# The statistics pass of the gate/up loop, moved from in front of a unit's evacuation to behind it

## The chip, the cores and the metric

The kernel runs on one core of one Trainium2 chip. The metric is the device time of one execution in microseconds (us), smaller is better. Executions of one kernel spread over 4.6 us here (the fastest of the kernel before took 765.78 us, the slowest 770.36 us), so differences of 0.2% need several rounds.

## The reference

Only the second half matters here: a gated feed-forward block whose two wide matrix products, gate and up, form the loop that the change edits. Shapes: 2048 tokens, D = 1024, F = 3584, all bf16.

```python
def _B_ref(x, w_gate, w_up, w_down):
    g = _silu(x @ w_gate)
    u = x @ w_up
    return (g * u) @ w_down

xn = _layernorm(A_x)
s = _A_ref(xn, A_wqkv, A_wo)            # linear attention block
g = _silu(_B_ref(xn, B_w_gate, B_w_up, B_w_down))
return A_x + s * g
```

## The kernel before

The feed-forward products use a Strassen-like scheme with seven products in place of eight. It needs differences of weight blocks in fp16, and these are scaled by a power of two so that they fit. The scale comes from a *statistics pass* over the raw weight tile: ScalarE squares it and sums per partition (`emit_st0`), TensorE adds over the partitions with a matrix of ones (`emit_st1`), VectorE makes the scale and applies it (`emit_st2`), GpSimd forms the four differences and writes the prepared tile to HBM for the second pass over the tokens (`emit_T`).

```python
def emit_st0(key, t):                                   # ScalarE
    asum = stp.tile([P, 1], BF16, name="asum", tag="asum")
    ...                                                 # cut: junk is a free part of the tile
    nc.scalar.activation(out=junk, in_=raw_view(key, t), func=ACT.Square, accum_out=asum[:])

def emit_a(key):                                        # first four products of a unit, then s1..s3
    ...
    nc.scalar.activation(out=s1[:], in_=x_[:], func=ACT.Copy, scale=rc)      # "the s1 copy", L752
    ...

def emit_evac(key, h, tail=None):                       # evacuation of a unit
    p, kind, fg = key
    ...
    if kind == "g":
        ...
        nc.scalar.activation(out=sg[:, 3, :], in_=s3[:], func=ACT.Silu)            # L799
        nc.scalar.activation(out=sg[:, 0, :], in_=x_[:], func=ACT.Silu, scale=rc)  # L800
        nc.scalar.activation(out=sg[:, 1:3, :], in_=cf[:], func=ACT.Silu)          # L801
    else:
        ...                                             # VectorE only
```

Units alternate: even i is a gate unit (`"g"`), odd i an up unit (`"u"`), 28 units of about 6.07 us. The loop of the first pass, cut to the order of issue:

```python
keys = [(p, kd, fg) for fg in range(NFG) for kd in ("g", "u")]
n = len(keys)                                           # 28

def raw(j):
    return 0 <= j < n and keys[j] in raw_keys           # not prepared in an earlier stage

def pipe(j):                                            # the statistics pass
    if raw(j):
        emit_st0(keys[j], w_tiles[keys[j]])
...
for i in range(n):
    load_w_to(...)                                      # cut
    if i + 1 < n:
        emit_a(keys[i + 1])
        emit_c22(keys[i + 1])
    for j in (range(5) if i == 0 else (i + 4,) if i != n - 6 else ()):
        pipe(j)
    if first:
        wd_pipe(i)          # down weights: a Square (i % 3 == 1) or a Copy that scales (i % 3 == 0)
        ...
    mb = emit_b(keys[i])                                # last three products of the unit
    if first and i in range(6, 11):
        io_load(mb)                                     # small loads of x and s for much later
    pipe1(i + (4 if i == n - 5 else 3), i)              # ones-matmul of the pass of a unit ago
    ...
    emit_evac(keys[i], h, tail if i == n - 1 else None)
    pipe2(i + (4 if i == n - 5 else 3))                 # scale and differences
    ...
```

All gate weights and up group 0 are prepared in an earlier stage of the kernel (`NPREP = 13` and the two first keys), so the raw keys are the 13 up keys 3, 5, ..., 27.

Of the kernel before, what the change touches and what calls it, by code (L numbers as in the profile page):

```python
# [21 lines left out]
def kernel(  # L22
# [179 lines left out]
    def raw_view(key, t):  # L202
        return wd_q(t)[:, 0:4:3, :] if key[1] == "w" else t[:, 0].rearrange("p a b -> p (a b)")
# [30 lines left out]
    def kcol(key):  # L234
        return 2 * NFG + key[2] if key[1] == "w" else 2 * key[2] + (1 if key[1] == "u" else 0)
# [7 lines left out]
    def emit_st0(key, t):  # L243
        asum = stp.tile([P, 1], BF16, name="asum", tag="asum")
        with nc.allow_low_precision("a bound that only sets a power of two"):
            junk = wd_q(t)[:, 1:3, :] if key[1] == "w" else t[:, 1].rearrange("p a b -> p (a b)")
            nc.scalar.activation(out=junk, in_=raw_view(key, t), func=ACT.Square, accum_out=asum[:])  # L247
        st_tiles[key] = asum

    def emit_st1(key, ps):  # L250
        nc.tensor.matmul(ps, lhsT=ones[:], rhs=st_tiles.pop(key)[:], start=True, stop=True, skip_group_check=True)
        st_tiles[key] = ps
# [459 lines left out]
    with ExitStack() as p3:  # L712
# [19 lines left out]
        def rc_of(key):  # L732
            if key[1] == "u" and key[0] != passes[0]:
                return rcl[:, key[2]:key[2] + 1]
            return rc_all[:, kcol(key):kcol(key) + 1]
# [45 lines left out]
        def emit_evac(key, h, tail=None):  # L781
            p, kind, fg = key
            x_, zw, s2, s3, _, *c = grp.pop(key)
            rc = rc_of(key)
            if kind == "g":
                cf = m4.tile([P, 2, TB], FP32, name="cg", tag="m4")
                d12 = cf[:]
            else:
                c = c[0]
                d12 = c[:, 0:2, :]  # L790
                sg = sg_tiles.pop((p, fg))
                nc.vector.scalar_tensor_tensor(out=h[:, 2 * fg, 0:TB], in0=x_[:], scalar=rc, in1=sg[:, 0, :],
                                               op0=ALU.mult, op1=ALU.mult)
            nc.vector.scalar_tensor_tensor(out=d12, in0=zw[:], scalar=rc,  # L794
                                           in1=s2[:, None, :].to_broadcast([P, 2, TB]), op0=ALU.mult, op1=ALU.add)
            if kind == "g":
                sg = m4.tile([P, 4, TB], BF16, name="sg", tag="m4")
                sg_tiles[(p, fg)] = sg
# [4 lines that stand above are left out]
                if tail is not None:  # L803
                    tail()
                hv = h[:, 2 * fg:2 * fg + 2, :].rearrange("p a b -> p (a b)")
                nc.vector.tensor_tensor(out=hv[:, TB:4 * TB], in0=c[:].rearrange("p a b -> p (a b)"),
                                        in1=sg[:, 1:4, :].rearrange("p a b -> p (a b)"), op=ALU.mult)
# [259 lines left out]
        for pi, p in enumerate(passes):  # L1067
            h = hp.tile([P, FC, TB2], BF16, name="hT", tag="hT")
            keys = [(p, kd, fg) for fg in range(NFG) for kd in ("g", "u")]
            n = len(keys)  # L1070
            first = pi == 0
            last_pass = pi == NPASS - 1

            if first:
                first_gate[0] = marks[("S", NB - 1, 0)]

            def raw(j):
                return 0 <= j < n and keys[j] in raw_keys

            def pipe(j):  # L1080
                if raw(j):
                    emit_st0(keys[j], w_tiles[keys[j]])

            def pipe1(k, i):
                if raw(k):
                    emit_st1(keys[k], grp[keys[i + 1]][4][:, 0:1])

            def pipe2(j):
                if raw(j):
                    t = w_tiles[keys[j]]  # L1090
                    emit_st2(keys[j], t, later=j == n - 1)
                    emit_lk(keys[j][2])
                    if j < n - 1:
                        emit_T(keys[j], t)
                    raw_keys.discard(keys[j])

            wd_live = {}

            def wd_pipe(i):
                if (i - 3) % 3 == 0 and i // 3 - 1 in wd_live:  # L1100
                    key, t = wd_live[i // 3 - 1]
                    w = raw_view(key, t)
                    nc.scalar.activation(out=w, in_=w, func=ACT.Copy, scale=cs_all[:, kcol(key):kcol(key) + 1])
                if (i - 1) % 3 == 0 and (i - 1) // 3 in wd_live:
                    emit_st0(*wd_live[(i - 1) // 3])

            def wd_pipe1(i):
                if (i - 2) % 3 == 0 and (i - 2) // 3 in wd_live:
                    emit_st1(wd_live[(i - 2) // 3][0], grp[keys[i + 1]][4][:, 1:2])

            def wd_pipe2(i):
                m, r = divmod(i + 1, 3)
                if r == 1 and m - 1 in wd_live:
                    emit_T(*wd_live[m - 1])
                elif r == 0:
                    if m - 1 in wd_live:
                        emit_st2(*wd_live[m - 1], later=True)
                    if NWE + m < NFG:
                        t = w_slot()
                        load_wd(t, NWE + m)  # L1120
                        wd_live[m] = ((p, "w", NWE + m), t)

            def more_S(m):
                if first:
                    scale_h(h, 2 * m, nc.scalar)
                    scale_h(h, 2 * m + 1, nc.vector)
                emit_hs(h, 0, m, nc.vector)

            def next_S(m):
                emit_hs(h, 1, m, nc.vector)  # L1130

            def tail():
                emit_hs(h, 0, 2, nc.vector)
                if first:
                    scale_h(h, 7, nc.scalar)
                emit_hs(h, 0, 3, nc.vector)

            na0 = 6 if first else 8
            load_w_to(base + na0)
            if first:  # L1140
                wd_pipe2(-1)
            emit_a(keys[0])
            emit_c22(keys[0])
            first_gate[0] = None
            for i in range(n):
                load_w_to(base + i + (na0 if i < n - 7 else 8 if i > n - 6 or not first else 7))
                if i + 1 < n:
                    emit_a(keys[i + 1])
                    emit_c22(keys[i + 1])
                for j in (range(5) if i == 0 else (i + 4,) if i != n - 6 else ()):  # L1150
                    pipe(j)
                if first:
                    wd_pipe(i)
                    for k in {n - 4: (0,), n - 3: (2, 4), n - 2: (5, 6)}.get(i, ()):
                        scale_h(h, k, nc.scalar)
                mb = emit_b(keys[i])
                if first and i in range(6, 11):
                    io_load(mb)
                pipe1(i + (4 if i == n - 5 else 3), i)
                if first:  # L1160
                    wd_pipe1(i)
                if i == n - 2:
                    emit_hs(h, 0, 0, nc.gpsimd)
                if i == n - 1:
                    emit_hs(h, 0, 1, nc.vector)
                emit_evac(keys[i], h, tail if i == n - 1 else None)
                pipe2(i + (4 if i == n - 5 else 3))
                if first:
                    wd_pipe2(i)
                    if i == 5:  # L1170
                        emit_lk(0)
                    if i == n - 5:
                        emit_lam()
                    elif i == n - 4:
                        emit_sc(keys[-1], w_tiles[keys[-1]])
                        emit_T(keys[-1], w_tiles[keys[-1]])
                        scale_h(h, 1, nc.vector)
                    elif i == n - 3:
                        scale_h(h, 3, nc.vector)
                if deferred:  # L1180
                    deferred.pop(0)()
            base += n
            emit_down(p, h, base, last_pass, more_S, next_S)
            base += 2 * NWA
# [32 lines left out]
```

## Time and profile before

| | before |
|---|---|
| median of the first 3 runs | 767.11 us (766.46 to 768.77) |
| span of the profiled execution | 767.3 us |
| TensorE (PE) busy | 754.1 us, 98% |
| ScalarE (ACT) busy | 345.8 us, 45% |
| PE gaps in the first gate/up loop | 1.15 us, one gap |

What to look for are the gaps of the busiest engine, and what ends them. From the page of the kernel before, part 1 (busy us of each engine) and part 4 (the chain that ended last):

```profile
PE 754.1 (98%) x3717; PEld 349.6 (46%) x3717; DVE 551.5 (72%) x1076; ACT 345.8 (45%) x473; POOL 287.4 (37%) x413
...
PE 92%; DVE 4%; ACT 1%; DMA 1%; issue 1%; SPq 0%; ACTq 0%; DVEq 0%
```

PE sets the time. The windows view of the kernel before, three stretches of the loop (length, then busy us and instructions of PE, PEld, DVE, ACT and POOL, then granted clock, DMA share, GB/s):

```profile
300.00:320.00 20.00, 20.00 (x96) 9.06 (x94) 17.21 (x28) 14.19 (x16) 17.62 (x18) 1.00 0.82 286
320.00:340.00 20.00, 18.85 (x90) 8.46 (x89) 15.11 (x28) 10.69 (x15) 10.47 (x12) 1.00 1.02 376
340.00:360.00 20.00, 20.00 (x97) 9.06 (x96) 16.45 (x27) 14.40 (x17) 18.20 (x19) 1.00 0.69 240
```

PE is full but for 1.15 us between 320 and 340 us, where the DMA engines are busiest of the three (share 1.02, against 0.82 and 0.69). The only wait of PE there, from the waits view of the kernel before (waiter, what it waited for, us in total, times, longest):

```profile
PE xb L725 <- ACT sg L800: 1.1, 1, 1.1
```

Two pieces of the ScalarE timeline of the kernel before (start, us, engine, line, operation; in brackets the idle time before it and what ended it). L247 is the statistics pass, L1103 the scaling Copy of down weights, L752 the s1 copy, L799 to L801 the Silus:

```profile
275.71 0.67 ACT L752 ACTIVATE s<-xb,rc_all 128x512 f32<-128x512 f32 x1
276.28 1.90 ACT L247 ACTIVATE w_sb<-w_sb 128x2048 bf16<-128x2048 bf16 x1
278.08 0.19 ACT L247 ACTIVATION_READ_ACCUMULATOR w_sb<-w_sb 128x1 bf16 x1
278.17 1.99 ACT L1103 ACTIVATE w_sb<-w_sb,cs_all 128x2048 bf16<-128x2048 bf16 x1
281.31 0.69 ACT L752 ACTIVATE s<-xb,rc_all 128x512 f32<-128x512 f32 x1 [1.15 <-PE xb L725]
...
324.23 0.67 ACT L752 ACTIVATE s<-xb,rc_all 128x512 f32<-128x512 f32 x1
330.63 1.91 ACT L247 ACTIVATE w_sb<-w_sb 128x2048 bf16<-128x2048 bf16 x1 [5.72 <-DMA w_sb<-in_B_w_up_dram]
332.44 0.19 ACT L247 ACTIVATION_READ_ACCUMULATOR w_sb<-w_sb 128x1 bf16 x1
332.54 0.67 ACT L752 ACTIVATE s<-xb,rc_all 128x512 f32<-128x512 f32 x1
333.11 1.99 ACT L1103 ACTIVATE w_sb<-w_sb,cs_all 128x2048 bf16<-128x2048 bf16 x1
335.00 0.62 ACT L799 ACTIVATE sg<-s 128x512 bf16<-128x512 f32 x1
335.52 0.67 ACT L800 ACTIVATE sg<-xb,rc_all 128x512 bf16<-128x512 f32 x1
```

The first piece is up unit 3: the pass, the Copy, then 1.15 us of idle until PE has the next operand. No Silu follows before that, because an up unit has none. The second piece is up unit 11: ScalarE stands in front of the pass for 5.72 us until the weights of key 15 have landed. The s1 copy behind it is late, and so is the Silu of L800, which frees a PSUM buffer that PE waits for. ScalarE ran nothing that stood behind the pass in those 5.72 us: the s1 copy came right after the pass, at 332.54 us, 8.31 us after the last one, where it is 5.60 us in the first piece.

### The profile page before, as it was taken

The numbers are of one execution on the slowest core, as the hardware profiler recorded it, in microseconds if no ns is written. First come the engines' busy times: TensorE is split into PE (matmuls) and PEld (weight loads), VectorE is DVE, ScalarE is ACT, GpSimd is POOL, SyncE is SP. The second block draws the span as 40 slices with busy tenths as digits, with TensorE's granted clock in tenths as the row PEclk, the third lists the DMA queues.
The fourth block names the chain that finished last, engine by engine and source line by source line (L and its number), as shares of the span: only waits on it lengthen the run. The fifth ranks groups of instructions, "written<-read, shape, count | busy, mean of one in ns | idle before, by whom it ended". The sixth has DMA issues, their size and how long they took to land.

```text
span 767.3 us, 10482 instructions
## 1 busy us (share of the span) xinstructions
PE 754.1 (98%) x3717; PEld 349.6 (46%) x3717; DVE 551.5 (72%) x1076; ACT 345.8 (45%) x473; POOL 287.4 (37%) x413
## 2 busy tenths in 40 slices
PE   7999999999999999999999999999999999999996
PEld 3544444444444444444444444444444444444443
DVE  6788557997666588878889885358676776787335
ACT  3545667788853566566447411132323223201111
POOL 0477499959685255858656000110000000200000
PEclk9999999999999999999999999999999999999999
DMA  9945868769889769898888227399654444530923
GB/s 308 352 95 114 229 221 274 248 222 259 237 304 262 256 228 312 283 333 298 308 309 290 89 81 262 113 356 334 229 185 167 165 169 175 187 114 23 296 73 117
DMA packets 105396, 170.29 MB, mean 222 GB/s; under 512 B 34688, under 2 KB 82176, under 8 KB 94720
## 3 DMA queue, kind: packets, MB, share of 16 engines
q1 hardware_dynamic: 94960, 121.00, 50.3%
q0 software_dynamic: 7936, 44.31, 15.0%
q10 hardware_dynamic: 2448, 4.33, 1.6%
q8 instruction: 29, 0.48, 0.3%
q14 instruction: 23, 0.19, 0.1%
HBM read 111.67 MB, written 50.59 MB: 211 GB/s over the span
## 4 chain that ended last, share of the span: by engine, by line
PE 92%; DVE 4%; ACT 1%; DMA 1%; issue 1%; SPq 0%; ACTq 0%; DVEq 0%
PE zw L725 25%; PE kv_ps L486 14%; PE dzw L910 13%; PE xb L725 12%; PE s_ps L659 7%; PE yb L725 6%; PE dx L910 6%; PE q_ps L170 4%; PE dy L910 3%; PE kvz L508 1%; DMA xp<-in_A_x_dram 1%; DVE o_blk L640 1%; PE nd_ps L632 1%; DVE pqT L141 1%; DVE pqT L153 0%
## 5 line engine op out<-in xcount | busy, mean ns | idle before, releaser
L725 PEld LDWEIGHTS <-w_sb 128*128 128x128 f16 (+1 forms) x1568 | 152.2, 98 | 184.3 <-issue 1.7
L725 PE MATMUL xb<-xnT,w_sb 128*128 128x512 bf16 x448 | 115.0, 379 | 1.1 <-ACT sg L800 1.1
L486 PE MATMUL kv_ps<-wkv_sb,xnT 128*128 128x512 bf16 x512 | 115.5, 383 | 0.4 <-DVE xnT L473 0.2
L725 PE MATMUL zw<-xnT,w_sb 128*128 128x512 bf16 x448 | 105.8, 379 | 0.0
L725 PE MATMUL zw<-S,w_sb 128*128 128x512 f16 x448 | 105.8, 379 | 0.0
L280 POOL TENSOR_TENSOR w_sb<-w_sb 128x512 f16<-128x512 bf16 x42 | 48.9, 1165 | 96.7 <-DVE w_sb L268 36.3
L247 ACT ACTIVATE w_sb<-w_sb 128x2048 bf16<-128x2048 bf16 x42 | 79.9, 1902 | 9.1 <-DMA w_sb<-in_B_w_up_dram 7.1
L910 PE MATMUL dx<-w_sb,hT 128*128 128x512 bf16 x224 | 82.8, 379 | 0.0
L486 PEld LDWEIGHTS <-xnT 128*128 128x128 bf16 x512 | 49.0, 98 | 57.2 <-issue 2.4
L910 PEld LDWEIGHTS <-hT 128*128 128x128 bf16 (+1 forms) x448 | 43.8, 98 | 52.9
L910 PE MATMUL dzw<-w_sb,hT 128*128 128x512 f16 (+1 forms) x224 | 64.4, 379 | 0.0
L170 PE MATMUL q_ps<-xnT,wq_sb 128*128 128x512 bf16 x256 | 58.2, 379 | 0.0
L753 DVE SCALAR_TENSOR_TENSOR s<-yb,rc_all,s 128x512 f32<-128x512 f32 x42 | 31.5, 749 | 37.0 <-ACT s L752 37.0
L659 PE MATMUL s_ps<-wo_sb,oT 128*128 128x512 bf16 x256 | 57.8, 379 | 0.0
L725 PE MATMUL yb<-S,w_sb 128*128 128x512 f16 x224 | 57.4, 379 | 0.0
L801 ACT ACTIVATE sg<-cg 128x1024 bf16<-128x1024 f32 x28 | 29.6, 1057 | 56.6 <-DVE cg L794 56.6
L794 DVE SCALAR_TENSOR_TENSOR cg<-zw,rc_all,s 128x1024 f32<-128x1024 f32 x28 | 35.9, 1283 | 25.4 <-PE zw L725 14.0
L850 POOL TENSOR_TENSOR hs<-hT 128x512 f16<-128x512 bf16 x2 | 2.5, 1258 | 132.6 <-ACT sg L801 132.6
L281 POOL TENSOR_TENSOR w_sb<-w_sb 128x512 f16<-128x512 bf16 x42 | 50.1, 1193 | 3.3
L283 POOL TENSOR_TENSOR w_sb<-w_sb 128x512 f16<-128x512 bf16 x42 | 50.8, 1210 | 0.0
L282 POOL TENSOR_TENSOR w_sb<-w_sb 128x512 f16<-128x512 bf16 x42 | 49.8, 1186 | 0.0
L884 POOL DMA_DIRECT2D out_dram<-io x16 | 8.7, 542 | 101.9 <-DVE io L883 101.6
(148 smaller groups left out, 1099.3 us busy)
## 6 DMA issues: line engine op xcount, KB each, us to landing
w_sb<-pk_g SPq DMA_DIRECT2D x27, 1024.0 KB, 6.0
pk_g<-w_sb POOLq DMA_DIRECT2D x14, 1024.0 KB, 5.4
pk_u<-w_sb POOLq DMA_DIRECT2D x14, 1024.0 KB, 6.4
w_sb<-wd SPq DMA_DIRECT2D x14, 1024.0 KB, 5.0
w_sb<-pk_u SPq DMA_DIRECT2D x14, 1024.0 KB, 4.9
w_sb<-wd SPq DMA_DIRECT2D x14, 768.0 KB, 5.8
w_sb<-in_B_w_gate_dram SPq DMA_DIRECT2D x14, 512.0 KB, 5.3
w_sb<-in_B_w_down_dram SPq DMA_DIRECT2D x28, 256.0 KB, 4.5
```

Source lines behind the costliest of these rows:

```text
L170: nc.tensor.matmul(q_ps[:], lhsT=wq_sb[:, dc, g * P:(g + 1) * P], rhs=xn_ap(dc, btok), start=(dc == 0), stop=(dc == DC - 1))
L247: nc.scalar.activation(out=junk, in_=raw_view(key, t), func=ACT.Square, accum_out=asum[:])
L280: nc.gpsimd.tensor_tensor(out=T1, in0=b12, in1=b11, op=ALU.subtract)
L281: nc.gpsimd.tensor_tensor(out=T2, in0=b22, in1=T1, op=ALU.subtract)
L282: nc.gpsimd.tensor_tensor(out=T3, in0=b22, in1=b12, op=ALU.subtract)
L283: nc.gpsimd.tensor_tensor(out=T4, in0=b21, in1=T2, op=ALU.subtract)
L486: mm = nc.tensor.matmul(kv_ps[:], lhsT=xn_ap(dc, tok), rhs=wkv_sb[:, dc, c * CW:(c + 1) * CW], start=(dc == 0), stop=(dc == DC - 1))
L659: mm = nc.tensor.matmul(s_ps[:], lhsT=oT[:, c, ttok], rhs=wo_sb[:, c, cc * CW:(cc + 1) * CW], start=(c == 0), stop=(c == G - 1))
L725: mm = nc.tensor.matmul(out, lhsT=lhs(k), rhs=rhs(k), start=(first and k == 0), stop=(k == HK - 1), skip_group_check=True)
L753: nc.vector.scalar_tensor_tensor(out=s2[:], in0=y_[:], scalar=rc, in1=s1[:], op0=ALU.mult, op1=ALU.add)
L794: nc.vector.scalar_tensor_tensor(out=d12, in0=zw[:], scalar=rc, in1=s2[:, None, :].to_broadcast([P, 2, TB]), op0=ALU.mult, op1=ALU.add)
L910: nc.tensor.matmul(out, lhsT=lhs, rhs=rhs, start=first, stop=lastk, skip_group_check=True)
```

## The change

The intent is to let the evacuation of a unit, which frees PSUM buffers, go first on ScalarE, and to run the statistics pass for a later unit behind it. The whole diff:

```diff
-                for j in (range(5) if i == 0 else (i + 4,) if i != n - 6 else ()):
+                for j in (range(4) if i == 0 else (i + 4,) if i == n - 5 else ()):
                     pipe(j)
 ...
                 emit_evac(keys[i], h, tail if i == n - 1 else None)
+                if i < n - 6:
+                    pipe(i + 4)
                 pipe2(i + (4 if i == n - 5 else 3))
```

## The prediction

> **What bounds it.** TensorE. The page of the profile has PE busy 754.1 of 767.3 us (98%), and PE is 92% of the chain that ended last. In the table by windows, the first gate/up loop (256 to 420 us), the only place that the edit touches, has PE busy in every 20 us stretch but one: 320 to 340 us holds 18.85 us. The waits name the gap: 1.1 us, "xb" on the ScalarE Silu of `sg[:,0]`.
>
> **What the change does.** In the source it moves a 1.90 us pass (Square, 128x2048 bf16, plus 0.19 us for the accumulator) from in front of a unit's evacuation to behind it. But it only acts where keys[i+4] is raw. All gate weights and up group 0 were prepared earlier, so raw keys are odd, so i is odd: an up unit. An up unit's evacuation has no ScalarE instruction; its Silus belong to the gate units. So the pass has nothing to step behind except the down-weight side work. Comparing the two compiled instruction orders confirms it: all other engines in identical order; on ScalarE six adjacent pairs swap and nothing else. At i = 1, 7, 13 the up pass and a down-weight Square (both 1.90 us) swap; at i = 3, 9, 15 the up pass and the down-weight Copy (1.99 us) swap.
>
> [...]
>
> **Cost.** Nothing is added or removed; each pair ends about when it did.
> - i = 3, 9, 15: the Copy moves up 1.9 us, then waits for its scale from VectorE (ready 276.6 and 313.0 in the timeline), so the pair ends 0.1 to 0.6 us later (estimate). The next ScalarE instruction came after 1.14 to 1.15 us of idle, waiting for PE: absorbed. The up pass ends about 2 us later; its consumer, the ones-matmul, comes about 5 us after that.
> - The GpSimd differences that need the Copy don't start sooner: they start (281.64, 318.11, 355.95) right behind GpSimd's own DMA issue. So write-backs, slot releases and loads stay.
> - i = 7, 13: before, the up pass idled 0.95 and 1.01 us for its operand; the down-weight pass may fill that, for nobody's gain.
> - The one PE gap comes from i = 11: the up pass waits 5.72 us for its DMA (until 330.63), which delays the next s1 copy, a Copy and the Silu. No pair swaps there, so it stays.
>
> **On the critical path:** 0 us; 1.15 us of PE gap that may vary with DMA congestion (DMA share 1.02 in that stretch).
>
> **Prediction:** 767.0 us, 8 in 10 within 765.4 to 768.8. Faster by over 2%: 0.01; within 2%: 0.98; slower by over 2%: 0.01.
>
> **What would show it.** Right: PE busy near 754 us; at 276 to 281 us ScalarE runs Copy, then Square; the GpSimd differences start within 0.3 us of before; the wait of 5 to 6 us for the up-weight DMA and the PE gap near 335 us are still there. Wrong: new PE gaps in 264 to 360 us.
>
> **What would make it wrong.** The Copy's scale arriving later than I read; at i = 7 or 13 the down-weight tile landing later than the up tile, so that the s1 copy is held and the yb/xb buffers run out, as at i = 11; or DMA timing moving the 1.15 us gap.

The forecast's sum was 0 us on the critical path; 1.90 and 1.99 us are read from the timeline of the kernel before.

## The result

In the first comparison the changed kernel took 767.76 us (median of 4 runs, 766.12 to 768.03) against 767.8 us before (4 runs). Ratios in this document are the mean time of one kernel's runs over that of the other's of the same rounds, so they are not quite the ratio of the medians. Here the ratio is 0.9996, with a 95% interval of 0.9974 to 1.0019: the same time.

The page of the changed kernel, parts 1 and 4:

```profile
PE 752.5 (98%) x3717; PEld 349.3 (46%) x3717; DVE 551.5 (72%) x1076; ACT 345.8 (45%) x473; POOL 287.7 (38%) x413
...
PE 87%; DVE 5%; DMA 5%; ACT 2%; issue 1%; SPq 1%; DVEq 0%; ACTq 0%
```

The chain has 5% of DMA here, against 1% before; 2% are the load of the raw up weights, which the next views explain. In the repeat below it is 1% again.

The windows view of the changed kernel, the one stretch in which PE is not full:

```profile
320.00:340.00 20.00, 18.33 (x88) 8.21 (x87) 15.43 (x28) 11.57 (x13) 9.95 (x11) 1.00 0.97 361
```

The waits of PE in the loop, changed kernel:

```profile
PE xb L725 <- ACT sg L800: 1.2, 1, 1.2
PE yb L251 <- DVE s L753: 0.5, 1, 0.5
```

The ScalarE timeline of the changed kernel, units 3 and 11 again. This execution runs 1.75 us ahead of the other when it enters the loop (275.71 against 273.96 us for the same s1 copy). The lead comes from before the edit: in the first 20 us the granted clock was 1.00 here and 0.91 there, about 1.8 us by an estimate from these figures (20 x 0.09).

```profile
273.96 0.67 ACT L752 ACTIVATE s<-xb,rc_all 128x512 f32<-128x512 f32 x1
274.97 2.00 ACT L1103 ACTIVATE w_sb<-w_sb,cs_all 128x2048 bf16<-128x2048 bf16 x1 [0.34 <-DVE cs_all L261]
276.88 1.89 ACT L247 ACTIVATE w_sb<-w_sb 128x2048 bf16<-128x2048 bf16 x1
278.68 0.19 ACT L247 ACTIVATION_READ_ACCUMULATOR w_sb<-w_sb 128x1 bf16 x1
279.56 0.69 ACT L752 ACTIVATE s<-xb,rc_all 128x512 f32<-128x512 f32 x1 [0.69 <-PE xb L725]
...
322.48 0.67 ACT L752 ACTIVATE s<-xb,rc_all 128x512 f32<-128x512 f32 x1
329.40 1.91 ACT L247 ACTIVATE w_sb<-w_sb 128x2048 bf16<-128x2048 bf16 x1 [6.25 <-DMA w_sb<-in_B_w_up_dram]
```

In unit 3 the pass and the Copy have swapped. The Copy waits 0.34 us for its scale, so the pair ends later and the idle time behind it shrinks from 1.15 to 0.69 us, but the next s1 copy still comes exactly when PE is ready: 5.60 us after the last one, as before (281.31 - 275.71 and 279.56 - 273.96). In unit 11 nothing has moved, and ScalarE stands before the pass for 6.25 us. The loop gained nothing and lost 0.5 us in this execution, as the weights landed 0.5 us later relative to the s1 copy.

GpSimd, whose differences need the Copy, starts them at the same place too. The timeline of GpSimd in the kernel before, its own DMA issue and then the differences of the down weights of unit 3:

```profile
281.05 0.57 POOL L293 DMA_DIRECT2D pk_u<-w_sb  x1 [0.30 <-POOL w_sb L283]
281.64 1.17 POOL L280 TENSOR_TENSOR w_sb<-w_sb 128x512 f16<-128x512 bf16 x1
```

The same in the changed kernel:

```profile
279.30 0.57 POOL L293 DMA_DIRECT2D pk_u<-w_sb  x1 [0.30 <-POOL w_sb L283]
279.89 1.18 POOL L280 TENSOR_TENSOR w_sb<-w_sb 128x512 f16<-128x512 bf16 x1
```

281.64 - 279.89 is 1.75 us, the offset between the two executions: the Copy came 1.45 us sooner relative to the rest (278.17 - 274.97 - 1.75) and GpSimd had no use for it.

### The profile page after: what moved, and what is told of

The parts are those of the page before. It is cut to its first block, busy times and chain, and to the rows that moved or that the text cites. A ratio compares the mean times of both kernels' runs of the same rounds, so it can differ in the third digit from the quotient of the medians.

```text
span 766.2 us, 10485 instructions
## 1 busy us (share of the span) xinstructions
PE 752.5 (98%) x3717; PEld 349.3 (46%) x3717; DVE 551.5 (72%) x1076; ACT 345.8 (45%) x473; POOL 287.7 (38%) x413
## 4 chain that ended last, share of the span: by engine, by line
PE 87%; DVE 5%; DMA 5%; ACT 2%; issue 1%; SPq 1%; DVEq 0%; ACTq 0%
PE zw L725 23%; PE kv_ps L486 13%; PE xb L725 12%; PE dzw L910 11%; PE s_ps L659 7%; PE yb L725 6%; PE dx L910 6%; PE q_ps L170 4%; PE dy L910 3%; DMA w_sb<-in_B_w_up_dram 2%; PE kvz L508 1%; DMA io<-s_dram 1%; DMA xp<-in_A_x_dram 1%; DVE o_blk L640 1%; DMA wd<-w_sb 1%
## 5 line engine op out<-in xcount | busy, mean ns | idle before, releaser
L486 PE MATMUL kv_ps<-wkv_sb,xnT 128*128 128x512 bf16 x512 | 113.8, 379 | 0.7 <-ACT r_t L151 0.4
L281 POOL TENSOR_TENSOR w_sb<-w_sb 128x512 f16<-128x512 bf16 x42 | 50.1, 1193 | 3.3
```

Of the source, the lines that this page charges most:

```text
L281: nc.gpsimd.tensor_tensor(out=T2, in0=b22, in1=T1, op=ALU.subtract)
L486: mm = nc.tensor.matmul(kv_ps[:], lhsT=xn_ap(dc, tok), rhs=wkv_sb[:, dc, c * CW:(c + 1) * CW], start=(dc == 0), stop=(dc == DC - 1))
```

## The experiments

The theory: the six swapped pairs are all the change does, nobody waits for either half of a pair, and PE is full; so the time should not move. Its rivals: the order has a real effect hidden in the noise; the passes do hold up the evacuations; or the place of the pass never matters because ScalarE is idle half of the time. A second question was what makes the one PE gap. Eleven runs were made, all with correct results.

### The changed kernel again, five rounds

No edit.

> The changed kernel once more, five rounds. Theory (the six swaps on ScalarE move nothing that anybody waits for): ratio to before 1.000, within 0.2%. Rival A (a small gain of the new order is real but was hidden by noise): 0.998 or lower, clear of 1. Rival B (the new order makes the one PE gap near 330 us larger, 1.7 us against 1.2 us): 1.0005 to 1.001.

Measured: 767.67 us (6 runs) against 767.71 us (11 runs), ratio 0.9998, interval 0.9979 to 1.0017. Neither rival gets support: no gain clear of noise and no loss. The windows view of this execution, over the whole loop:

```profile
255.00:440.00 185.00, 185.00 (x876) 84.05 (x874) 155.34 (x263) 113.80 (x123) 105.24 (x105) 1.00 0.76 269
```

PE is busy for all of 185.00 us: the gap is not there, in the same kernel that had 1.67 us of it in its first profile. So the gap comes and goes between executions of one kernel, and rival B, which was drawn from one profile against one other, loses its ground (the interval alone would still allow its 1.0005 to 1.001).

### The pass nearly taken away

The edit, shortened (the run has an argument for the number of columns, which only the passes of the loop set):

```diff
-            nc.scalar.activation(out=junk, in_=raw_view(key, t), func=ACT.Square, accum_out=asum[:])
+            nc.scalar.activation(out=junk[:, 0:16], in_=src[:, 0:16], func=ACT.Square,
+                                 scale=(2048 / 16) ** 0.5, accum_out=asum[:])   # raw up keys of the loop only
```

> Kernel before, but the statistics pass over the raw up weights in the gate/up loop reads 16 of 2048 columns (scaled, so the bound is about the same), under 0.4 us instead of 1.9 us, 12 times: about 20 us of ScalarE work gone. Theory: the pass is off the critical path, so PE busy stays and the time stays within 0.2% of before; only the gap near 330 us, which is a wait for the weight's DMA and not for the pass, may shrink by up to 1.2 us. Rival (the pass holds up the evacuations, so its place matters): 5 to 20 us faster.

Measured: 766.35 us against 767.71 us, ratio 0.9985, interval 0.9965 to 1.0005. ScalarE busy falls from 345.8 to 324.4 us. That is 21.4 us, from 13 passes and not 12 as written above. PE is busy for 185.00 us in the loop, and the pass at unit 11 waits 1.98 us for its weights. Removing nearly all of the work (an ACTIVATE of 0.21 us is left, and 0.19 us for reading the accumulator) bought 1.4 us by the medians, not clear of noise, and 2.7 us at the far end of the interval (0.0035 x 767.7). No place of this pass should be worth more than having next to no pass; so this bounds the change from above. (The sampled sum is no true bound on the weights, so this is no kernel to keep.)

### The small loads of x and s moved away

```diff
-                if first and i in range(6, 11):
+                if first and i in range(17, 22):
                     io_load(mb)
```

> Kernel before, but the ten small loads of x and s (io) that are issued in units 6 to 10 are issued in units 17 to 21. Theory (the one PE gap comes from the up weights of key 15 landing late, behind crowded DMA work): those weights land by about 325 us, ScalarE waits under 1 us instead of 5.7 us at unit 11, the PE gap near 335 us is gone, 1 us (0.15%) faster. Rival (those loads are not what delays it): ScalarE still waits about 5 us for them and the gap stays.

Measured: 767.21 us against 767.71 us, ratio 0.9996, interval 0.9977 to 1.0016. The ScalarE timeline of this kernel at unit 11:

```profile
324.77 0.67 ACT L752 ACTIVATE s<-xb,rc_all 128x512 f32<-128x512 f32 x1
325.34 1.90 ACT L247 ACTIVATE w_sb<-w_sb 128x2048 bf16<-128x2048 bf16 x1
327.14 0.19 ACT L247 ACTIVATION_READ_ACCUMULATOR w_sb<-w_sb 128x1 bf16 x1
330.36 0.69 ACT L752 ACTIVATE s<-xb,rc_all 128x512 f32<-128x512 f32 x1 [3.02 <-issue]
```

The wait of 5.72 us is gone and PE is full in the loop (185.00 us busy in 255 to 440 us). That is what the theory expected of the trace; the expected 1 us does not show in the time. Nor do the gaps settle the cause: the changed kernel lost its gap once without this edit. The gap was absent in both executions profiled with the later loads (this one and the last experiment), and present in two of the four executions profiled with the loads in their old place and a pass of no more than its usual length in unit 11 (there in both kernels' first profiles, not in the repeat, nor with the small pass).

The DMA view says more. With the loads in their old place, the weights of key 15 took 12.0 us from issue to landing (kernel before), 12.6 and 9.2 us (changed kernel, first profile and repeat), 8.9 us (small pass), 11.4 and 8.9 us (the next two experiments). With the loads moved they took 7.1 us here and 7.8 us in the last experiment. They were also issued 5.7 to 6.4 us ahead of the s1 copy that the pass follows in unit 11 in the first six executions, and 8.2 and 7.6 us ahead in the other two. Six executions against two do not overlap, so in these profiles the small loads do delay the weights. Why the time varies from 8.9 to 12.6 us with the loads in place is not shown.

### The pass of key 15 alone held back

```diff
-                for j in (range(5) if i == 0 else (i + 4,) if i != n - 6 else ()):
+                for j in (range(5) if i == 0 else () if i in (11, n - 6) else (i + 3,) if i == 12 else (i + 4,)):
```

> Kernel before, but the pass over key 15 alone is issued in unit 12, behind the next copy of xb to SBUF, instead of in unit 11. Theory (PE's gap arises because ScalarE, in order, stands before this pass for 5.7 us while the copy, the Copy and the Silu behind it are ready): the copy runs about 3 us earlier, the PE gap of 1.15 us shrinks or goes, 0.5 to 1.1 us faster. Rival (PE waits for something else there, such as the weights themselves): the gap stays at 1.1 us or more.

Measured: 766.9 us against 767.71 us, ratio 0.9995, interval 0.9975 to 1.0015. The s1 copy that had stood behind it came at its usual time (327.88 us, 5.59 us after the last one; in the kernel before it was 8.31 us after, 332.54 - 324.23). The PE gap shrank from 1.1 to 0.5 us but did not go, because the pass now stands directly before the Copy and the Silus of gate unit 12. This was not an execution with early weights: they landed 11.4 us after issue, at about 327.8 us (316.42 + 11.4), so in its old place the pass would have stood for some 4.9 us behind the s1 copy that ended at 322.96 us (an estimate from these figures). This fits the theory that ScalarE, held by a pass that waits for its weights, passes the delay on to PE. It is one profile, and the time shows nothing.

### The passes issued in gate units, in front of the Silus

```diff
-                for j in (range(5) if i == 0 else (i + 4,) if i != n - 6 else ()):
+                for j in (range(4) if i == 0 else (i + 3,) if i % 2 == 0 and i <= n - 6
+                          else (i + 4,) if i == n - 5 else ()):
```

> Kernel before, but each pass over raw up weights is issued in the following gate unit (3 units ahead of use instead of 4), in front of that unit's evacuation with its three Silus. Theory: it delays the Silus by up to 2.1 us, in the units that also hold a down-weight pass up to the PE gap: within 0.5% of before, 0 to 4 us slower; the DMA wait at unit 11 disappears from ScalarE.

Measured: 769.98 us against 767.61 us, ratio 1.0032, interval 1.001 to 1.0055: 0.3% slower, as expected. Here the pass does stand before Silus, and the waits of PE in the loop say what it costs:

```profile
PE xb L725 <- ACT sg L800: 3.0, 6, 0.5
```

Six gaps of 0.5 us, 3.0 us in all, against a measured 2.5 us (0.0032 x 767.6). So a pass in front of an evacuation can cost PE time; in the kernel before, the passes of the loop are issued in up units, where there are no Silus behind them.

### The passes issued in gate units, behind the Silus

The edit against the kernel before. In this run and in the last one the ones-matmul of a pass comes in the same unit as the pass, and no longer a unit later:

```diff
-                for j in (range(5) if i == 0 else (i + 4,) if i != n - 6 else ()):
+                for j in (range(4) if i == 0 else (i + 4,) if i == n - 5 else ()):
 ...
-                pipe1(i + (4 if i == n - 5 else 3), i)
+                late_pass = i % 2 == 0 and 2 <= i <= n - 6
+                if not late_pass:
+                    pipe1(i + (4 if i == n - 5 else 3), i)
 ...
                 emit_evac(keys[i], h, tail if i == n - 1 else None)
+                if late_pass:
+                    pipe(i + 3)
+                    pipe1(i + 3, i)
```

> As gate_front, but the pass is issued behind that gate unit's evacuation, which is what the words of the change describe, with its ones-matmul in the same place on PE. Theory: the pass can now start only after the last Silu, 2.4 us after PE has finished the unit, and PE's ones-matmul waits for it: 4 to 5 us of PE gap in each of 11 units, 40 to 55 us slower (5 to 7%). Rival (place in the order never matters, ScalarE has time enough): within 0.5% of before.

Measured: 840.19 us against 767.61 us, ratio 1.0945, interval 1.0918 to 1.0972: 9.5% slower. The rival that place never matters is out. (A pass behind the Silus whose ones-matmul comes a unit later was not tried, so this run does not say what the place alone costs.) The direction was as expected, the size was not (40 to 55 us expected, 72.6 us measured). The waits of PE in the loop, this kernel:

```profile
PE yb L251 <- ACT w_sb L247: 47.9, 11, 4.4
```

One of these gaps in the PE timeline of this kernel, with the matmuls behind it (start, us, line, operation, count, idle before):

```profile
275.75 0.16 PE L251 MATMUL yb<-asum,ones 128*128 128x1 bf16 x1 [4.36 <-ACT w_sb L247]
275.77 1.87 PE L725 MATMUL yb<-S,w_sb 128*128 128x512 f16 x4
277.43 1.91 PE L725 MATMUL xb<-xnT,w_sb 128*128 128x512 bf16 x4
279.14 2.57 PE L725 MATMUL zw<-S,w_sb 128*128 128x512 f16 x8
281.55 1.03 PE L725 MATMUL xb<-xnT,w_sb 128*128 128x512 bf16 x4
```

One stretch of the windows view of this kernel:

```profile
320.00:360.00 40.00, 31.29 (x130) 13.26 (x129) 23.27 (x36) 14.84 (x17) 22.80 (x22) 0.87 0.75 252
```

The gaps are as expected, 11 of 4.4 us, 47.9 us. What the expectation left out is the clock: after the gap two groups of four matmuls take 1.87 us and 1.91 us, where such a group takes 1.03 us later in the same unit, and the granted clock of the stretch is 0.87. The profiled execution spans 69.6 us more than that of the kernel before (836.9 against 767.3): PE busy grows from 754.1 to 777.9 us, so slower matmuls add 23.8 us, and PE's idle time adds the other 45.8 us. In the gap shown above the granted clock (0.87 on average from 256 to 280 us) was 1.00 until 273.5 us and 0.50 from 274.0 us, some 2.1 to 2.6 us after PE had stopped (275.75 - 4.36 = 271.39). It was still 0.50 from 275.75 to 280.50 us, and 1.00 from 281.50 us on. The next experiment has shorter gaps with a clock of 0.50 behind them. Behind the single gap of 1.15 us in the kernel before the clock stayed at 1.00 (stretch of 320 to 340 us).

### The passes tripled, in both orders

The edit, shortened (`times` is an argument that only the passes of the loop set):

```diff
+            for _ in range(times):                      # 3 for raw up keys of the loop
                 nc.scalar.activation(out=junk, in_=raw_view(key, t), func=ACT.Square, accum_out=asum[:])
```

> Kernel before, with each statistics pass over raw up weights in the gate/up loop run three times in a row (same result): 12 times 3.8 us more ScalarE work, 46 us in all. Theory: most of it falls into ScalarE's idle time (3.0 us in up units without down-weight work, 1.1 us in those with it); what is over delays the next copy by 0.8 to 2.7 us, and PE forgave 1.5 us of such delay at unit 11. So PE gaps of about 1 us in six units and 4 to 5 us at unit 11: 5 to 15 us slower. Rival (the passes are on the critical path): 40 us or more slower.

> The changed kernel with the same tripled passes. Theory: where ScalarE has no slack left the order of a pair still decides only when each of the two is done, not the pair: within 0.3% of the tripled kernel before. Rival (the new order helps once ScalarE is short of time, since the down-weight Copy and with it the GpSimd differences no longer wait behind 5.7 us of passes): 3 us or more faster than the tripled kernel before.

Measured, 3 rounds: 783.26 us with the order of before (ratio 1.0193, interval 1.0165 to 1.022) and 785.87 us with the order of the change (1.023, 1.0203 to 1.0256). So the passes cost time when they are three times as long, but far less than the 50.1 us by which ScalarE busy grew (395.9 - 345.8, 13 passes of 3.85 us). It was a little more than the 5 to 15 us expected, and the two orders differed by 0.4% (1.023 over 1.0193) with overlapping runs. Both were run again.

> The kernel before with tripled passes once more, beside the next run, five rounds, since the two differed by 0.4% with overlapping runs. Theory (the order inside a pair does not matter even without slack; the difference came from the granted clock of single executions): 1.019 to 1.023 of before.

> The changed kernel with tripled passes once more. Theory: within 0.2% of the tripled kernel before of this call, in either direction. Rival (without slack the new order costs, since the up pass ends one down-weight pass later and its consumer on PE waits): again 0.3% or more slower than it.

Measured, 5 rounds: 784.49 us (ratio 1.0223, interval 1.0202 to 1.0244) and 783.82 us (1.0222, 1.0206 to 1.0239). The orders agree within the intervals even with ScalarE busy for 155.96 of the 185 us of the loop (112.88 in the kernel before), and neither rival (the new order faster in the first call, slower in the second) finds support. The 0.4% of the first call goes with the granted clock, as was expected before the second: its mean over the runs was 0.9968 and 0.9935 in the first call, 0.9948 and 0.9958 in the second. Of the 17 tripled runs the two at a clock of 0.999 took 781.5 and 782.3 us, the three at 0.991 took 786.3 to 787.4 us. Where the time goes, from the waits of PE in the loop, tripled passes in the order of before, second call (lines are one higher here, since the edit adds a line):

```profile
PE yb L252 <- ACT w_sb L248: 5.4, 2, 2.9
PE xb L726 <- ACT sg L801: 3.5, 3, 1.2
PE yb L252 <- DVE s L754: 2.8, 4, 1.8
PE zw L726 <- DVE cg L795: 1.2, 2, 0.9
...
```

PE is busy for 171.10 us of the 185 in the loop in this order and for 171.20 us in the other: 13.9 and 13.8 us of gaps. The largest term, 5.4 us in two waits, is what the expectation had missed. The passes of keys 3 and 27 are issued in the unit in which their ones-matmul comes (units 0 and 23), so there a longer pass is felt at once. The change moves neither.

The two gaps of that term also bear on the clock. PE waited 2.9 us for the pass of key 27 in all four tripled executions, and each time the clock fell to 0.50 (its mean over the loop was 0.98 in both executions with the order of before and 0.99 in both with that of the change). It waited 2.4 us for the pass of key 3; the windows behind that gap, in the order of before (gap until 262.51 us) and in that of the change (until 261.61 us), second call (the third number from the end is the granted clock):

```profile
263.00:264.00 1.00, 1.00 (x4) 0.44 (x3) 0.78 (x3) 1.00 (x2) 0.00 (x0) 0.50 0.26 76
262.00:263.00 1.00, 1.00 (x7) 0.46 (x5) 0.77 (x3) 1.00 (x3) 0.00 (x0) 1.00 0.40 118
```

The first call shows the same pair. So a gap of 2.4 us was followed by a lower clock in two executions and not in two others; whether the order or chance decided it, four executions do not say. In the second call's profile of the order of before, slower matmuls make up 3.8 us (757.9 - 754.1 of PE busy) of the 16.5 us by which the span grew (783.8 - 767.3).

### The changed kernel with the small loads moved

The changed kernel, with the edit of the loads shown above.

> The changed kernel with the small loads of x and s issued in units 17 to 21: the best candidate. Theory: no PE gap in the gate/up loop (185.00 us busy in the stretch from 255 to 440 us), ScalarE never waits over 2.5 us for weights there, and a time 0 to 1.2 us below before, which the spread of single executions (4 us) hides: ratio 0.998 to 1.001.

Measured: 766.0 us (6 runs) against 767.41 us (11 runs), ratio 0.9987, interval 0.9974 to 1.0. PE is full in the loop, 185.00 us, and all statistics passes of the kernel together wait 1.2 us for weights, in three waits. This is the fastest of the kernels with a proper statistics pass, but by 0.13%, with an interval that touches 1, and the same edit on the kernel before gave 0.9996. No version with the full pass is clearly faster than the kernel before.

## Why the prediction was right

It gave 767.0 us within 765.4 to 768.8, and 98% for "within 2%"; measured were 767.76 us at first and 767.67 us in the repeat.

- *The change acts only in up units, which have no ScalarE evacuation.* Right. The compiled order shows six swapped pairs on ScalarE and identical order elsewhere. The traces show the three of pass and Copy (units 3, 9 and 15; the first is shown above); the three pairs of two like Squares cannot be told apart in them. The words of the change describe a move that happens nowhere; what was moved were passes against down-weight work.
- *Each pair ends about when it did, at most 0.6 us later, absorbed by idle time.* Right: the Copy waited 0.34 us, the idle time went from 1.15 to 0.69 us, and the next s1 copy kept its 5.60 us.
- *GpSimd does not start sooner.* Right: at units 3 and 9 the shift is the 1.75 us offset of the execution, no more (281.64 and 279.89; 318.11 and 316.36), and at unit 15 it is the 1.23 us that are left behind the larger PE gap (355.95 and 354.72).
- *At units 7 and 13 the down-weight pass fills the up pass's wait, for nobody's gain.* The waits there are gone in the first profile of the changed kernel. That nobody gained follows from the time, and from the passes being worth about 1.4 us as a whole.
- *The one PE gap stays.* Half right. It was there in the first profile (1.67 us in place of 1.15 us) and absent in the next profile of the same kernel. The prediction allowed for drift with DMA timing; it should have said that one profile can't tell such a gap from a property of the kernel.
- *0 us on the critical path.* Right, and the experiments say why it isn't luck: with almost no pass the time falls by 0.15%, with tripled passes the two orders still agree (1.0223 and 1.0222). The ones-matmul of a pass comes a whole unit after the pass; that slack is why its place is free. Without it, in front of the Silus, the cost was 0.3%; without it and behind the Silus, 9.5%.

What stays open is what else makes the weights of key 15 late in some executions. Moving the small loads brings them sooner (7.1 and 7.8 us to landing, against 8.9 to 12.6 us), but with the loads in place the gap was there in two executions and vanished in two. The changed kernel alone had 12.6 and 9.2 us for the same weights in its two profiles, and ScalarE waited 6.25 us for them in the one and 2.45 us in the other.

## What to carry to other kernels

Before costing a reorder, work out for which iterations the moved statement does anything, and compare the compiled order of each engine: here a condition on the key confined it to units in which there was nothing to step behind. Here a step with a unit of slack before its consumer was moved by the length of one instruction and nothing came of it; the same step behind an evacuation, with its consumer next on PE, cost a gap of 4.4 us in each of 11 units, and 2.2 us more each from the lower TensorE clock (23.8 / 11). A bound on what a reorder can gain is the run with the work taken out, and it is cheap to measure.
